# A two-layer linear-attention block: phi(q) loaded with its 32-token blocks side by side, M's rows in a matching order, the square's high part on ScalarE

## The chip, the cores and the metric

The kernel runs on one NeuronCore of a Trainium2 chip. The metric is the device time of one execution in microseconds (us). A kernel's time is the median of several executions. The profile is one further execution, recorded by the hardware profiler; its span goes from the first to the last instruction, and its own time is a little longer than the span.

## What is computed

The input x has 2048 tokens of 640 features in float32. Two layers, with the same weights, each do:

```
phi(t) = where(t > 0, t + 1, exp(t)) + 1e-6
q, k, v = layernorm(x) @ wqkv                      # 32 heads of 20
kv = phi(k)^T v  per head;   z = sum over tokens of phi(k)
o  = (phi(q) kv) / (phi(q) . z + 1e-6)             # per head
x  = x + o @ wo
h  = relu(layernorm(x) @ w1 + b1)
x  = x + (h * h) @ w2 + b2                         # 640 -> 1728 -> 640
```

The kernel merges the block-diagonal kv with wo: M = kv @ wo is a 640 x 640 matrix, and the attention output is (phi(q) / den) @ M.

Nearly all matmuls multiply float32 values in three passes. Each operand is split into a high part (rounded to the matmul's type) and a low part (the value less its high part), and high x low, low x high and high x high are summed in PSUM. So each operand of a matmul costs one copy (high) and one subtraction (low) on other engines.

## The kernel before

**Tiling.** The 2048 tokens are 16 tiles of 128 (`NT`), the 640 features are 5 chunks of 128 (`DC`), the 1728 hidden features 14 chunks (`NF`, the last of 64). For the feed-forward part the tiles go in 4 groups of 4 (`TG`, `NG`).

**Stages of a layer.** First the k and q projections over all tiles, with the sums for kv; phi(q) of each tile is stored to memory (`pqd[t]`), for some tiles in "late" quarters (`late_q`, each 15 matmuls of 320 columns) that are placed later as work for TensorE. Then the transition: the sum z is spread over all partitions (`zbc`), kv and M are made (`kv_make`, `m_make`), M is split into high and low (`m_split`), and the first four tiles (group 0) are projected through M, added to x and normalised. Then the feed-forward part, group by group: for each of 14 chunks `fc1` (15 matmuls of 512 columns), `act` (Relu, square, split), and `fc2` of the chunk before (15 matmuls of 512). Beside group g's chunks the kernel does the attention output of group g+1, two tiles at a time, by a scheme of seven products instead of eight (`Pair`, `p1` to `p7`), which takes sums and differences of M's row chunks and of the turned phi(q).

**What sets the order.** The order is written by hand: each engine works through its instructions in the order in which the program emits them. Beside the feed-forward part, `pair_plan`, `fast`, `OUT0`, `OUTS` and `STRIP` say at which chunk and at which place of it ("pre", after the i-th tile of `fc2`, "pe", "post") each step of a pair is emitted (`side`, `run`). All DMAs but one are issued by SyncE, in program order, and a DMA that waits holds up those behind it. The tiles come from rings; `ftile` is one of 12 tiles of 128x640.

**phi(q) of a tile, from memory to the projection.** `b_load_pq` loads the stored tile, tokens on partitions. `b_ops` multiplies it by `zbc` (L626), sums per head (L629), adds and inverts (L635, L636), scales the tile (L638), and turns it: a projection needs features on partitions. `blocks_T` (L375) is one VectorE transpose, which turns each 32x32 block in place; `blocks_move` then puts the 16 blocks of a 128x128 square where they belong, with 16 ScalarE copies of 32 partitions x 160 per tile (L388). The result is split by `split` or `p_split`. The moves are handed out in quarters (`side_moves` and `run_side` in the transition, `moves0` and `moves1` of a plan in the feed-forward part). The normalised tiles that feed `fc1` go through the same two steps; these stay as they are.

**M.** `m_make(c)` makes 120 rows of M (6 heads; 40 rows for the last of 6 pieces) in PSUM; ScalarE copies them out. Piece 0 goes straight into `m_raw[0]`; the others go to an `ftile` and are laid into the 128-row tiles `m_raw[0..4]` by one or two DMAs each:

```
m, r = divmod(o, P)
k = min(P - r, n)
nc.sync.dma_start(m_raw[m][r : r + k], u[:k])
if k < n:
    nc.sync.dma_start(m_raw[m + 1][: n - k], u[k:n])
```

`m_split(m)` makes the high part (L984) and the low part (L985), both on VectorE. The first projections use M[0] to M[2] (`proj(..., range(3))`), then M[3] and M[4]. Between the pieces and behind them stand late quarters: one after piece 2, two after piece 5. Eight subtractions of M's halves (`m_sums`) feed the seven-product scheme, four on GpSimd and four on VectorE.

**act.** ScalarE takes the Relu from PSUM (L1141), VectorE squares it (L1142), casts the high part (L1143) and takes the low part (L1144).

Of the kernel before, what the change touches and what calls it, by code (L numbers as in the profile page):

```python
# [13 lines left out]
P = 128  # L14
# [33 lines left out]
def pair_plan(b, m0, m1, turn, out, back):  # L48

    return {"moves0": m0, "moves1": m1, "turn": turn, "out": out, "back": back}  # L50


def fast(b, m0=None, m1=None):
    return pair_plan(
        b, m0 or (b - 3, 0), m1 or (b - 2, 0), [(b - 1, 0), (b - 1, 1), (b - 1, 2), (b - 1, 3)],
        {"p1": (b, 0), "p4": (b, 1), "p6": (b, 2), "p7": (b, 3), "p5": (b, 4),
         "p2": (b + 1, 0), "p3": (b + 1, 2)},
        [((b, "post"), (b + 1, 0), (b + 1, 1), (b + 2, 0), (b + 2, 1), (b + 2, 3)),
         ((b + 1, 3), (b + 1, "post"), (b + 2, 0), (b + 2, "post"), (b + 3, "pre"), (b + 3, 4))],
    )  # L60
# [7 lines left out]
OUTS = ({**fast(2), ("den", 1): ((-1, 1), (-1, 3))}, fast(9))  # L68
# [7 lines left out]
def kernel(  # L76
# [87 lines left out]
    def utile(name):  # L164
        return tmp.tile([P, 2 * D], R32, tag="u", name=name, bufs=RING)

# [288 lines left out]
    for layer in range(N_LAYERS):  # L455
# [167 lines left out]
        def b_ops(t):  # L623

            pr = ftile("pr")
            nc.vector.tensor_tensor(out=pr, in0=pq[t], in1=zbc, op=ALU.mult)  # L626
# [14 lines left out]
            yield  # L641
            yzp[t] = blocks_T(pq.pop(t))
# [13 lines left out]
        def b_split(t, u):  # L656
            split(u[:, 0], u[:, 1], yzp.pop(t)[1])
            pT[t] = chunks(u)
# [4 lines left out]
        def b_x1(t, ps, n=0):  # L663
            v = halves_sb(xr[t])
            nc.vector.tensor_tensor(out=v, in0=halves(ps), in1=v, op=ALU.add)
            if n:
                m_sum(n, xr[t][:, :1])
            b_norm(t)

        def b_norm(t):  # L670
            ln_stats(("b", t), xr[t])
            next(m_vec)
            xn[t] = ftile("xn")
            ln_apply(("b", t), xn[t], xr[t])
# [198 lines left out]
        zbc = tmp.tile([P, D], F32, tag="z", name="zbc", bufs=1)  # L873
# [6 lines left out]
        for j in range(2):  # L880
            nc.scalar.activation(zbc[:, j * HD : (j + 1) * HD], psz[j], AF.Copy)
# [16 lines left out]
        def side_moves(yz, then=None):  # L898
            side_work.extend(lambda k=k: blocks_move(yz, (k,)) for k in range(P // B32))
            if then:  # L900
                side_work.append(then)
# [33 lines left out]
        def m_make(c):  # L935
            mb.append(mb.pop(0))
            ps = bank(mb[-1], 2)
            n, o = head_rows(c), HR * c
            for j in range(2):
                nc.tensor.matmul(  # L940
                    ps[:n, j * 512 : j * 512 + HD], kvbd[c][:n, :n],
                    vo["o", c][:n, j * HD : (j + 1) * HD], start=True, stop=True,
                )

            u = m_raw[0] if c == 0 else ftile("Mc")
            nc.scalar.activation(halves_sb(u[:n]), halves(ps[:n]), AF.Copy)
            if c > 0:
                m, r = divmod(o, P)
                k = min(P - r, n)
                nc.sync.dma_start(m_raw[m][r : r + k], u[:k])  # L950
                if k < n:
                    nc.sync.dma_start(m_raw[m + 1][: n - k], u[k:n])

        def m_sums(m, engine):


            b1, b2, lo, hi = m_raw[m], m_raw[m + 2], slice(0, HD), slice(HD, D)
            for out, x, y in (
                (b1[:, lo], b1[:, hi], b1[:, lo]),
                (b1[:, hi], b2[:, hi], b1[:, hi]),  # L960
                (b2[:, hi], b2[:, hi], b1[:, lo]),
                (b2[:, lo], b2[:, lo], b2[:, hi]),
            ):
                engine.tensor_tensor(out=out, in0=x, in1=y, op=ALU.subtract)
                yield


        m_pool, m_vec = m_sums(0, nc.gpsimd), m_sums(1, nc.vector)
        W = (2, 1, 1, 0, 0)

        def m_sum(n, v):

            w = small.tile([P, 1], F32, tag="rs", name="rs")
            nc.gpsimd.tensor_copy(w, v)
            for _ in range(n):
                next(m_pool)

        def split_sum(t, n):
            u = xtile("pT")
            b_split(t, u)  # L980
            m_sum(n, u[:, 1, :1].bitcast(F32))

        def m_split(m):
            nc.vector.tensor_copy(M[m][:, 0], m_raw[m])  # L984
            nc.vector.tensor_tensor(  # L985
                out=M[m][:, 1], in0=m_raw[m], in1=M[m][:, 0].bitcast(F32), op=ALU.subtract
            )
# [24 lines left out]
        side_moves(yzp[2], lambda: split_sum(2, W[0]))  # L1012
# [12 lines left out]
        m_split(2)  # L1025
        late_q(1)
        run_side(1)
        m_split(3)

# [11 lines left out]
        for i in range(2):  # L1041
            po[i] = bank(4 + 2 * i, 2)
            proj(po[i], pT[i], M, range(3))
            if i == 0:
                m_split(4)
            run_side(2)
# [7 lines left out]
        def x_there(i):  # L1054
            f_split(i, yzx.pop(i)[1])
            if i == 0:
                m_sum(W[2], xTb[0][:, 1, 0, :1].bitcast(F32))

# [12 lines left out]
        for i in (2, 3):  # L1071
# [3 lines left out]
            b_x1(i, po[i], W[i + 1])  # L1075
            if i == 2:
                xbanks = [1, 2, 3]
            late_q(1)
            run_side(1)
        late_q(1)  # L1080
# [24 lines left out]
        )  # L1105

# [28 lines left out]

        def act(c, ps):
# [3 lines left out]
            if c < 13:  # L1140
                nc.scalar.activation(r, ps, AF.Relu, bias=b1sb[:, c : c + 1])  # L1141
                nc.vector.tensor_tensor(out=r, in0=r, in1=r, op=ALU.mult)  # L1142
                nc.vector.tensor_copy(h[:, 0], r)  # L1143
# [141 lines left out]
        def x1_tile():  # L1285
            return bp.tile([P, TG, D], F32, tag="x1", name="x1", bufs=1)

        def x1_load(g):
            x1s[g] = x1_tile()
# [4 lines left out]
        if layer == 0:  # L1294
            stage = x1_tile()
# [13 lines left out]
        def s_turns(t):  # L1309


            z0, z1 = yzp.pop(t)[1], yzp.pop(t + 1)[1]
# [20 lines left out]
        def p_split(t, first=0):  # L1333

            u = bp.tile([P, 2, D], R32, tag="pT", name="pT", bufs=2)
            v, s = yzp[t][1], slice(first * P, D)
# [125 lines left out]
        def side(g, p, plan, at):  # L1462

            t0, t1 = TG * g + 2 * p, TG * g + 2 * p + 1
            m0, m1, turn, out, back = plan["moves0"], plan["moves1"], plan["turn"], plan["out"], plan["back"]
            for t, (s, pl) in ((t0, m0), (t1, m1)):
                if t != TG:
                    at(s - 4, "post", lambda t=t: b_load_pq(t))
                den, blk = plan.get(("den", t - t0), ((s - 2, "post"), (s - 1, 1)))
                at(*den, lambda t=t: b_den(t))  # L1470
                at(*blk, lambda t=t: b_blocks(t))
                for k in range(4):
                    at(s + (pl + k) // 5, (pl + k) % 5, lambda t=t, k=k: blocks_move(yzp[t], (k,)))
            steps(at, lambda: p_split(t0), (m0[0] + 1, 0), (m0[0] + 1, 4))
            steps(at, lambda: p_split(t1, 2), (m1[0] + 1, 0), (m1[0] + 1, 1))
# [71 lines left out]

        pend = None
        for g in range(NG):
            for c in range(NF):  # L1550
# [4 lines left out]
                if last_layer and g == NG - 1 and c == NF - 2:  # L1555
                    hl = act(c + 1, fc1(g, c + 1, spare=True))
                    fc2(*pend)
# [3 lines left out]
                if pend:  # L1561
                    fc2(*pend, after=lambda i: run(g, c, i))
                    wu.load_ring()
                else:
                    for i in range(TG + 1):
                        run(g, c, i)
# [6 lines left out]
                if g == 0 and c < TG:  # L1573
                    f_bias(c)
# [38 lines left out]
```

## Time and profile before

| | us |
|---|---|
| median of 3 runs | 1345.48 |
| the three runs | 1344.94, 1345.48, 1345.90 |
| the profiled execution's own time | 1345.11 |
| its span | 1343.4 |
| first layer's feed-forward part begins | 252.67 |
| second layer's M begins | 874.21 |

How to read the lines below. The engines are PE (TensorE), PEld (its weight loads), DVE (VectorE), ACT (ScalarE), POOL (GpSimd) and SP (SyncE). In the page's first part stand busy time, share of the span and number of instructions of each. A group of instructions reads: line, engine, operation, output<-input by the program's names, shapes, count | busy us, mean ns of one | idle time before them and what ended it. A line of the timeline reads: start, duration, engine, line, operation, names and shapes, count, and in brackets the idle time before it with its releaser. A line of the stretches reads: from:to and length, then busy time and instructions of PE, PEld, DVE, ACT and POOL, the granted clock, the share of the DMA engines and GB/s. A line of TensorE's waits reads: who waited for whom, us in total, times, the longest. A DMA line reads: names, queue, count, KB of one, median us from issue to landing. A matmul's duration includes its way through the array, so matmuls overlap: their spacing is shorter than their duration.

### The profile page before, as it was taken

To read this page: it belongs to the slowest core of one execution; us is meant where nothing else is said; L and a number is where in the kernel's file an instruction comes from. 1 tells how busy PE (TensorE), PEld (TensorE's weight loads), DVE (VectorE), ACT (ScalarE), POOL (GpSimd) and SP (SyncE) were. 2 spreads that over 40 slices of the span, in tenths; PEclk is the share of its full clock that TensorE was granted. 3 is DMA by queue.
4 is the path that set the end of the run, shared out by engine and by line. 5 is a ranking of instruction groups with operands and counts; after the bars stand their busy time and mean duration, and the time that the engine had idled before them with its cause. 6 is when DMAs were issued, how large, how long until landed. Compare 5 with 4: busy or idle time off the path is not lost.

```text
span 1343.4 us, 19060 instructions
## 1 busy us (share of the span) xinstructions
PE 1336.3 (99%) x6746; PEld 1151.6 (86%) x6746; DVE 937.6 (70%) x1711; ACT 788.7 (59%) x1996; POOL 133.1 (10%) x185
## 2 busy tenths in 40 slices
PE   9999999999999999999999999999999999999998
PEld 8888999988888888888888899998888888888887
DVE  8888868887876776643467678678769767666323
ACT  5878848666647548512647686495657466474120
POOL 2222210100000000000012232110000000000000
PEclk9999999999999999999999999999999999999999
DMA  6787825474565575487621115156546556555635
GB/s 206 256 302 269 286 88 181 159 295 168 182 220 175 184 268 171 156 307 278 223 98 50 50 40 156 42 207 232 180 168 240 180 183 214 212 169 185 243 132 192
DMA packets 85637, 253.44 MB, mean 189 GB/s; under 512 B 11030, under 2 KB 19606, under 8 KB 84902
## 3 DMA queue, kind: packets, MB, share of 16 engines
q1 hardware_dynamic: 85398, 252.04, 53.7%
q8 instruction: 53, 0.87, 0.3%
q14 instruction: 42, 0.34, 0.1%
q10 hardware_dynamic: 144, 0.20, 0.0%
HBM read 193.50 MB, written 56.03 MB: 186 GB/s over the span
## 4 chain that ended last, share of the span: by engine, by line
PE 90%; DVE 7%; ACT 1%; DMA 1%; issue 1%; POOL 0%; SPq 0%; DVEq 0%
PE PS L400 36%; PE PS L1179 24%; PE PS L1130 24%; PE PS L421 2%; PE PS L927 1%; PE PS L940 1%; ACT z L388 1%; PE PS L736 1%; DVE y L375 1%; DMA pqt<-pq 1%; DVE hr L1142 0%; DVE x L1230 0%; DVE bn L355 0%; DVE pqt L638 0%; DVE pr L626 0%
## 5 line engine op out<-in xcount | busy, mean ns | idle before, releaser
L388 ACT ACTIVATE z<-y 32x160 f32<-32x160 f32 x1384 | 462.5, 334 | 65.2 <-DVE y L375 48.7
L1130 PE MATMUL PS<-xTb,u 128*128 128x512 f32 x1400 | 333.4, 390 | 0.6 <-DVE hr L1150 0.6
L1130 PEld LDWEIGHTS PS<-xTb,u 128*128 128x128 f32 x1400 | 262.0, 188 | 55.6 <-DVE hr L1150 1.5
L400 PE MATMUL PS<-kq,xT 128*128 128x320 f32 (+2 forms) x1575 | 284.5, 335 | 0.0
L1179 PE MATMUL PS<-u,h 128*128 128x512 f32 x1120 | 279.4, 390 | 0.0
L400 PEld LDWEIGHTS PS<-kq,xT 128*128 128x128 f32 x1575 | 250.3, 188 | 27.8 <-DVE rl L506 1.5
L1179 PEld LDWEIGHTS PS<-u,h 128*128 128x128 f32 x1120 | 207.9, 188 | 40.0
L1141 ACT ACTIVATE hr<-PS,b1sb 128x512 f32<-128x512 f32 x104 | 71.4, 686 | 276.0 <-PE PS L1130 275.2
L1142 DVE TENSOR_TENSOR hr<-hr 128x512 f32<-128x512 f32 x104 | 71.6, 688 | 186.2 <-ACT hr L1141 186.2
L400 PE MATMUL PS<-kh,xh 128*128 128x512 f32 x480 | 124.1, 392 | 0.0
L498 ACT ACTIVATE e<-PS 128x320 f32<-128x320 f32 (+4 forms) x128 | 53.5, 435 | 107.7 <-PE PS L400 99.3
L359 POOL TENSOR_SCALAR rs<-mv 128x1 f32<-128x1 f32 x63 | 29.7, 472 | 755.9 <-DVE mv L357 755.9
L400 PEld LDWEIGHTS PS<-kh,xh 128*128 128x128 f32 x480 | 87.1, 188 | 15.2 <-DVE kh L700 0.4
L505 DVE TENSOR_SCALAR e<-e 128x320 f32<-128x320 f32 (+4 forms) x128 | 41.6, 325 | 70.1 <-ACT e L498 69.9
L1179 PE MATMUL PS<-h,u 128*128 128x512 f32 x280 | 79.4, 391 | 0.2
L1144 DVE TENSOR_TENSOR h<-hr,h 128x512 fp32r<-128x512 f32 x104 | 72.0, 693 | 3.6
L697 POOL TENSOR_TENSOR acc<-acc,r 128x640 f32<-128x640 f32 x30 | 53.9, 1796 | 197.6 <-DVE r L506 197.6
L1179 PEld LDWEIGHTS PS<-h,u 128*128 128x128 f32 x280 | 51.9, 188 | 11.6 <-DVE strip L1195 1.0
L1130 PE MATMUL PS<-xTb,uw 128*128 128x512 f32 x240 | 57.0, 389 | 0.0
L506 DVE SCALAR_TENSOR_TENSOR r<-PS,e 128x512 f32<-128x512 f32 (+2 forms) x104 | 51.1, 491 | 5.8 <-ACT e L498 2.4
L1130 PEld LDWEIGHTS PS<-xTb,uw 128*128 128x128 f32 x240 | 45.1, 188 | 9.4
L1143 DVE CAST h<-hr 128x512 fp32r<-128x512 f32 x104 | 44.4, 427 | 7.8 <-DVE hr L1142 0.5
(137 smaller groups left out, 1525.7 us busy)
## 6 DMA issues: line engine op xcount, KB each, us to landing
u<-kept_w SPq DMA_DIRECT2D x184, 640.0 KB, 4.8
x<-x SPq DMA_DIRECT2D x48, 320.0 KB, 4.5
kept_w<-uprep SPq DMA_DIRECT2D x23, 640.0 KB, 5.3
pqt<-pq SPq DMA_DIRECT2D x32, 320.0 KB, 5.1
x<-xr SPq DMA_DIRECT2D x32, 320.0 KB, 2.4
st<-in_B_w_dram SPq DMA_DIRECT2D x22, 320.0 KB, 5.2
pq<-r SPq DMA_DIRECT2D x20, 320.0 KB
kept_kq<-kq SPq DMA_DIRECT2D x10, 640.0 KB, 5.8
```

The costliest lines, as they stand in the source:

```text
L388: nc.scalar.activation(d, v, AF.Copy)
L400: nc.tensor.matmul(ps, a, b, start=first and i == 0, stop=last and i == 2)
L498: nc.scalar.activation(self.e[:, a:b], ps, AF.Exp)
L505: nc.vector.tensor_scalar(e, e, 1.0, PHI_EPS, op0=ALU.min, op1=ALU.add)
L506: nc.vector.scalar_tensor_tensor(out=self.r[:, a:b], in0=ps, scalar=0.0, in1=e, op0=ALU.max, op1=ALU.add)
L697: nc.gpsimd.tensor_tensor(out=acc, in0=acc, in1=r, op=ALU.add)
L1130: nc.tensor.matmul(ps, a[:, d, :], bb[:, d, :], start=n == 0, stop=n == len(order) - 1)
L1141: nc.scalar.activation(r, ps, AF.Relu, bias=b1sb[:, c : c + 1])
L1142: nc.vector.tensor_tensor(out=r, in0=r, in1=r, op=ALU.mult)
L1143: nc.vector.tensor_copy(h[:, 0], r)
L1144: nc.vector.tensor_tensor(out=h[:, 1], in0=r, in1=h[:, 0].bitcast(F32), op=ALU.subtract)
L1179: nc.tensor.matmul(ps, l, r, start=first and k == 0, stop=last and k == len(a) - 1)
```

## The change

- `b_load_pq` loads a tile by four DMAs. Partition 32j + q gets, from tokens q, 32 + q, 64 + q and 96 + q, the features 160j to 160j + 159, side by side. The arithmetic of `b_ops` keeps its shapes in other views; `zbc` holds only the 160 sums that its partition needs, written in four pieces by ScalarE and VectorE.
- One VectorE transpose with a strided input then gives the whole turned tile, and the 16 ScalarE moves are gone for phi(q). Row 32j + b of feature chunk c now holds feature 160j + 32c + b instead of 128c + 32j + b.
- M's rows are put in the same order: each run of up to 32 rows of a piece goes by a DMA of its own to `m_raw[m][32j + ...]`. All six pieces go this way.
- `m_split`'s high part is made by ScalarE. The late quarters that stood between M's pieces and splits stand differently: none after piece 2, two right behind piece 5 and one behind the first three splits. All `m_sums` are on VectorE.
- `act`: ScalarE makes the square's high part directly from the Relu (function Square). VectorE's square and low part are emitted later, after the second tile of the following `fc2` (`LOW_AT`).
- The plans change: the first group's pairs start at chunks 4 and 9 instead of 5 and 10, the strips at chunk 6 instead of 8, and the slots for moves of phi(q) are gone. The `x1` tile and the first `pT` tile of the feed-forward pool are allocated when the pool opens.

The order of TensorE's matmuls changes with the plans and the late quarters; their number and shapes don't.

```diff
-OUT0 = (fast(5), {**fast(10, (5, 0), (8, 0)), ("vec", 0): (0,)})
+OUT0 = (fast(4), fast(9))
-STRIP = ((8, 0), (8, 2), (8, 4), (9, 0), (9, 2))
+STRIP = ((6, 0), (6, 2), (6, 4), (7, 0), (7, 2))
...
+    JB = P // B32
+    R_ = D // JB
...
         def b_load_pq(t):
                 pq[t] = ftile("pqt")
-                nc.sync.dma_start(pq[t], pqd[t])
+                v = pqd[t].rearrange("(i q) (j r) -> j q i r", i=JB, j=JB)
+                for j in range(JB):
+                    nc.sync.dma_start(
+                        pq[t][j * B32 : (j + 1) * B32].rearrange("q (i r) -> q i r", i=JB), v[j]
+                    )
...
-            nc.vector.tensor_tensor(out=pr, in0=pq[t], in1=zbc, op=ALU.mult)
+            nc.vector.tensor_tensor(
+                out=pr.rearrange("p (i r) -> p i r", i=JB),
+                in0=pq[t].rearrange("p (i r) -> p i r", i=JB),
+                in1=zbc[:, None, :].to_broadcast([P, JB, R_]), op=ALU.mult,
+            )
...
-            yzp[t] = blocks_T(pq.pop(t))
+            yzp[t] = z = ftile("z")
+            nc.vector.transpose(
+                out=z, in_=pq.pop(t).rearrange("p (i c b) -> p c i b", i=JB, b=B32)
+            )
...
-        side_moves(yzp[0], lambda: b_split(0, xtile("pT")))
+        b_split(0, xtile("pT"))
         b_den(1)
-        run_side(4)
         b_blocks(1)
-        side_moves(yzp[1], lambda: b_split(1, xtile("pT")))
+        side_work.append(lambda: b_split(1, xtile("pT")))
...
-            u = m_raw[0] if c == 0 else ftile("Mc")
+            u = ftile("Mc")
             nc.scalar.activation(halves_sb(u[:n]), halves(ps[:n]), AF.Copy)
...
+            r = o
+            while r < o + n:
+                k, b = divmod(r, B32)
+                l = min(B32 - b, o + n - r)
+                j, m = divmod(k, DC)
+                nc.sync.dma_start(m_raw[m][j * B32 + b : j * B32 + b + l], u[r - o : r - o + l])
+                r += l
...
         def m_split(m):
-            nc.vector.tensor_copy(M[m][:, 0], m_raw[m])
+            nc.scalar.activation(M[m][:, 0], m_raw[m], AF.Copy)
...
+        Q = (2, 1, 1, 1)
         for c in range(NH):
             m_make(c)
-            run_side(1)
+            if c > 2:
+                run_side(1)
             b_step(3)
-            if c == 2:
-                late_q(1)
-            if c in (3, 4):
-                m_split(c - 3)
-        side_moves(yzp[3], lambda: split_sum(3, W[1]))
+        side_work.append(lambda: b_split(3, xtile("pT")))
+        late_q(Q[0])
+        run_side(1)
+        for m in range(3):
+            m_split(m)
         late_q(1)
-        run_side(1)
-        m_split(2)
-        late_q(1)
-        run_side(1)
         m_split(3)
+        m_split(4)
+        m_sum(4)
...
             if c < 13:
                 nc.scalar.activation(r, ps, AF.Relu, bias=b1sb[:, c : c + 1])
-                nc.vector.tensor_tensor(out=r, in0=r, in1=r, op=ALU.mult)
-                nc.vector.tensor_copy(h[:, 0], r)
-                nc.vector.tensor_tensor(
-                    out=h[:, 1], in0=r, in1=h[:, 0].bitcast(F32), op=ALU.subtract
-                )
+                nc.scalar.activation(h[:, 0], r, AF.Square)
+
+                def rest():
+                    nc.vector.tensor_tensor(out=r, in0=r, in1=r, op=ALU.mult)
+                    nc.vector.tensor_tensor(
+                        out=h[:, 1], in0=r, in1=h[:, 0].bitcast(F32), op=ALU.subtract
+                    )
+
+                lows.append(rest)
```

More of the change, by code (lines that the diff above doesn't have):

```diff
@@ L671, in b_norm @@
             ln_stats(("b", t), xr[t])
-            next(m_vec)
+            m_sum(1)
             xn[t] = ftile("xn")
@@ L872 @@
         late_q(1)
-        zbc = tmp.tile([P, D], F32, tag="z", name="zbc", bufs=1)
+        zbc = tmp.tile([P, R_], F32, tag="z", name="zbc", bufs=1)
         psz = [xbank()[:, :HD] for _ in range(2)]
@@ L879 @@
                 )
-        for j in range(2):
-            nc.scalar.activation(zbc[:, j * HD : (j + 1) * HD], psz[j], AF.Copy)
+        for j in range(JB):
+            p, k = slice(j * B32, (j + 1) * B32), j % 2
+            v = psz[j // 2][p, k * R_ : (k + 1) * R_]
+            if k == 0:
+                nc.scalar.activation(zbc[p], v, AF.Copy)
+            else:
+                nc.vector.tensor_copy(zbc[p], v)
         b_den(0)
@@ L963, in m_sums, with m_sum @@
             ):
-                engine.tensor_tensor(out=out, in0=x, in1=y, op=ALU.subtract)
+                nc.vector.tensor_tensor(out=out, in0=x, in1=y, op=ALU.subtract)
                 yield
[L968 to L974, printed above, removed]
-            for _ in range(n):
[L976 to L981, printed above, removed]
+        m_turn = [m_sums(m) for m in range(2)]
+        def m_sum(n):
+            for _ in range(n):
+                next(m_turn[0])
         def m_split(m):
-            nc.vector.tensor_copy(M[m][:, 0], m_raw[m])
+            nc.scalar.activation(M[m][:, 0], m_raw[m], AF.Copy)
             nc.vector.tensor_tensor(
@@ L1105, with x1_tile, pT_tile @@
         )
+        def x1_tile():
+            return bp.tile([P, TG, D], F32, tag="x1", name="x1", bufs=1)
+        def pT_tile():
+            return bp.tile([P, 2, D], R32, tag="pT", name="pT", bufs=2)
+        x1_first, pT_first = [x1_tile()], [pT_tile()]
         def fresh(nm):
@@ L1134, in fc1, with low @@
             return ps
+        lows = []
+        def low():
+            if lows:
+                lows.pop(0)()
         def act(c, ps):
@@ L1333, in p_split @@
         def p_split(t, first=0):
-            u = bp.tile([P, 2, D], R32, tag="pT", name="pT", bufs=2)
-            v, s = yzp[t][1], slice(first * P, D)
+            u = pT_first.pop() if pT_first else pT_tile()
+            v, s = yzp[t], slice(first * P, D)
             nc.scalar.activation(u[:, 0, s], v[:, s], AF.Copy)
@@ L1464, in side @@
             t0, t1 = TG * g + 2 * p, TG * g + 2 * p + 1
-            m0, m1, turn, out, back = plan["moves0"], plan["moves1"], plan["turn"], plan["out"], plan["back"]
-            for t, (s, pl) in ((t0, m0), (t1, m1)):
+            m0, m1, turn, out, back = plan["blocks0"], plan["blocks1"], plan["turn"], plan["out"], plan["back"]
+            for t, s in ((t0, m0), (t1, m1)):
+                den, blk = plan.get(("den", t - t0), ((s - 1, "post"), (s, 1)))
                 if t != TG:
-                    at(s - 4, "post", lambda t=t: b_load_pq(t))
-                den, blk = plan.get(("den", t - t0), ((s - 2, "post"), (s - 1, 1)))
+                    at(den[0] - 2, "post", lambda t=t: b_load_pq(t))
                 at(*den, lambda t=t: b_den(t))
                 at(*blk, lambda t=t: b_blocks(t))
[L1472 to L1475, printed above, removed]
+            steps(at, lambda: p_split(t0), (m0 + 1, 0), (m0 + 1, 2))
+            steps(at, lambda: p_split(t1, 2), *plan.get("split1", ((m1 + 1, 0), (m1 + 1, 1))))
             steps(at, lambda: s_turns(t0), *turn)
@@ L1546, in side_last, with after @@
                 blocks_move(yz0[2], (2 * c - 24, 2 * c - 23))
+        def after(g, c, i):
+            if i == LOW_AT:
+                low()
+            run(g, c, i)
         pend = None
@@ L1565 @@
                     for i in range(TG + 1):
-                        run(g, c, i)
+                        after(g, c, i)
                 pend = g, c, h
```

66 lines of the change are left out of this document (30 added, 36 removed).

## The prediction

> **What bounds the kernel now.** I read the busy times first, then TensorE's own waits, then the few stretches that contain them.
>
> ```profile
> PE 1336.3 (99%) x6746; PEld 1151.6 (86%) x6746; DVE 937.6 (70%) x1711; ACT 788.7 (59%) x1996; POOL 133.1 (10%) x185
> ...
> PE PS L544 <- POOL ident masks.py:199: 1.4, 1, 1.4
> PE PS L400 <- DVE xr L1390: 0.8, 1, 0.8
> PE PS L1130 <- DVE hr L1150: 0.6, 2, 0.3
> ...
> 268.80:302.40 33.60, 32.79 (x160) 27.88 (x160) 28.05 (x51) 21.75 (x56) 0.79 (x2) 1.00 0.76 295
> 336.00:369.60 33.60, 33.27 (x159) 27.95 (x158) 27.89 (x51) 21.37 (x57) 1.58 (x4) 1.00 0.53 184
> 369.60:403.20 33.60, 33.49 (x166) 28.46 (x165) 24.70 (x46) 16.06 (x42) 1.58 (x4) 1.00 0.60 218
> 1008.00:1041.60 33.60, 33.19 (x148) 26.82 (x147) 30.65 (x55) 25.38 (x68) 0.79 (x2) 1.00 0.67 243
> 1310.40:1343.40 33.00, 29.20 (x131) 23.85 (x129) 11.62 (x20) 3.35 (x5) 0.00 (x0) 1.00 0.54 189
> ```
>
> TensorE is busy for 1336.3 of 1343.4 us, so 7.1 us are idle. The last stretch (33.00 less 29.20) holds 3.8 us, mostly the tail after the last matmul, and 1.6 us are waits at the start (1.4 for the identity and 0.2 for the first normalised tile). What is left for any change of order is 0.81 + 0.33 + 0.11 + 0.41 = 1.7 us. The change adds and removes no matmul; it moves the order of a few. So a lighter VectorE or ScalarE can buy at most about 1.7 us (0.13%), while any wait put in TensorE's way costs its full length. The whole question is whether the change makes such a wait.
>
> **Parts that lie beside other work.** These rows price them:
>
> ```profile
> L388 ACT ACTIVATE z<-y 32x160 f32<-32x160 f32 x1384 | 462.5, 334 | 65.2 <-DVE y L375 48.7 <-DMA x<-x 0.6
> L1141 ACT ACTIVATE hr<-PS,b1sb 128x512 f32<-128x512 f32 x104 | 71.4, 686 | 276.0 <-PE PS L1130 275.2
> L1143 DVE CAST h<-hr 128x512 fp32r<-128x512 f32 x104 | 44.4, 427 | 7.8 <-DVE hr L1142 0.5
> L375 DVE STREAM_TRANSPOSE y<-pqt 128x640 f32<-128x640 f32 x32 | 27.0, 844 | 1.0
> L964 POOL TENSOR_TENSOR Mr<-Mr 128x320 f32<-128x320 f32 x8 | 7.0, 880 | 0.5 <-DMA u<-kept_w 0.3
> pqt<-pq SPq DMA_DIRECT2D x32, 320.0 KB, 5.1
> ```
>
> Of the 1384 block moves, 504 go: 504 x 0.334 = 168 us off ScalarE. It gets 104 squares; the trace has no square, so between a cast's 0.43 (on another engine) and the Relu's 0.69 from PSUM; I take 0.69, 72 us. VectorE loses 104 x 0.427 = 44 us of casts and gets the eight 128x320 subtractions, which GpSimd did in 0.88 each (7 us at most). All of this lies under TensorE, which waits for neither engine except in the stretches above. The transpose now reads runs of 32 elements 160 apart. The trace has no such read: 0.84 us if the pattern is free, twice that if not; I take 0.84, because the ScalarE moves already read 32-wide pieces. The upper value would add 32 x 0.84 = 27 us to an engine that idles for 1343 - 938 = 406.
>
> Each load of a phi(q) tile becomes four DMAs of 32 partitions, 96 more on SyncE's queue. Landing took 5.1 us before and the loads are issued about two chunks (14 us) ahead of their use; at 0.4 to 0.9 us of issue each (rows below) a tile is complete 1.2 to 2.7 us later. The tight one is the second tile of group 1 in layer 0, whose chain ends in the 0.8 us wait on L1390. Its deadline moves up one chunk, but four slots of block moves leave the chain, so I keep that wait as it is (0 to 2.5 us).
>
> [...]
>
> The waits on L1150 (0.6 us) sit at the turn to group 1 in both layers, where VectorE is busiest; the plan of that pair ends one chunk earlier now and has 0.43 us less per chunk. I give the change the idle of those stretches, 0.33 + 0.11 + 0.41, so -0.9 us.
>
> **The part on the path: M's rows.** M is made in six pieces of 120 rows (40 in the last). Before, the first is copied straight into place and the others are laid into 128-row tiles by 9 DMAs per layer. Now the rows of each tile come from all over M, and no piece is copied straight: 4+5+5+4+4+2 = 24 DMAs per layer, all issued by SyncE one after the other. TensorE and SyncE in layer 0, and what the edits touch:
>
> ```profile
> 206.75 2.46 PE L400 MATMUL PS<-kq,xT 128*128 128x320 f32 x15
> 209.05 3.39 PE L940 MATMUL PS<-uraw,kvbd 120*120 120x320 f32 x12
> 217.93 4.67 PE L400 MATMUL PS<-kq,xT 128*128 128x320 f32 x30
> 222.44 13.40 PE L421 MATMUL PS<-uM,pT 128*128 128x320 f32 x90
> ...
> 210.33 0.70 ACT L946 ACTIVATE Mr<-PS 120x640 f32<-120x640 f32 x1 [0.64 <-PE PS L940]
> ...
> 200.43 0.49 DVE L506 SCALAR_TENSOR_TENSOR rl<-PS,e 128x320 f32<-128x320 f32 x1
> 200.84 0.81 DVE L626 TENSOR_TENSOR pr<-pqt,zbc 128x640 f32<-128x640 f32 x1
> 207.25 0.81 DVE L134 TENSOR_TENSOR pT<-z,pT 128x640 fp32r<-128x640 f32 x1
> 209.72 0.33 DVE L505 TENSOR_SCALAR e<-e 128x320 f32<-128x320 f32 x1 [0.32 <-ACT e L498]
> 210.08 0.49 DVE L506 SCALAR_TENSOR_TENSOR rl<-PS,e 128x320 f32<-128x320 f32 x1
> ...
> 210.60 0.33 SPq L867 DMA_DIRECT2D pq<-rl  x1
> 212.90 0.74 SPq L950 DMA_DIRECT2D Mr<-Mc  x1
> 213.70 0.61 SPq L952 DMA_DIRECT2D Mr<-Mc  x1
> 215.03 0.53 SPq L950 DMA_DIRECT2D Mr<-Mc  x1
> 215.61 0.87 SPq L952 DMA_DIRECT2D Mr<-Mc  x1
> 217.48 0.78 SPq L950 DMA_DIRECT2D Mr<-Mc  x1
> 218.31 0.55 SPq L952 DMA_DIRECT2D Mr<-Mc  x1
> 219.61 0.56 SPq L950 DMA_DIRECT2D Mr<-Mc  x1
> 220.26 0.83 SPq L952 DMA_DIRECT2D Mr<-Mc  x1
> ...
> Mr<-Mc SPq DMA_DIRECT2D x2, 240.0 KB, 2.8
> Mr<-Mc SPq DMA_DIRECT2D x2, 80.0 KB, 3.9
> ...
> L985 DVE TENSOR_TENSOR uM<-Mr,uM 128x640 fp32r<-128x640 f32 x10 | 8.3, 825 | 0.3
> L133 ACT ACTIVATE uT<-Mr 128x640 fp32r<-128x640 f32 x8 | 5.2, 730 | 0.0
> ```
>
> The deadline. TensorE makes M from 209.05 and starts the first projection at 222.44. Between these lie 45 late matmuls before and after, only placed differently, so the deadline stays 13.4 us after M's first matmul.
>
> The cost of an issue. In order, the rows are of 8, 112, 16, 104, 24, 96, 32 and 88 partitions. Those of 16, 32, 96 and 112 held SyncE 0.53 to 0.61 us, the others 0.74 to 0.87, while the store of the row above them took 0.33. From start to start this is about 0.58 for 16 partitions (215.03 to 215.61), 0.65 for 32 (219.61 to 220.26), 0.80 for 8, 0.83 for 24.
>
> When the queue starts. The first piece is copied at 211.03 (210.33 + 0.70). But the store in front on SyncE (210.60) waits for the late quarter's `rl` on VectorE (ready 210.57), and that comes later now: the low half of tile 0's phi(q) is taken right after 200.84 and waits there for ScalarE's high half (about 0.65), then costs 0.75 start to start; tile 1's takes the place it had at 207.25. Of these 1.4 us, 0.3 fall into VectorE's idle at 209.72. So `rl` is ready at 211.6, and the first M DMA starts at 212.05.
>
> When M[0] is there. Its last 32 rows are rows 480 to 511, the first DMA of the fifth piece, 19th in the queue. The 18 ahead of it: first piece 3 x 0.65 + 0.83 = 2.8; second 0.80 + 3 x 0.65 + 0.58 = 3.3; third the same 3.3; fourth 2.8; sum 12.2. It starts at 224.3 and lands 2.8 us later (the median of the 96-row DMA; the one 32-row value is 3.9), at 227.1. ScalarE's high part takes 0.73, so the projection starts at about 227.9 instead of 222.44: 5.4 us of idle TensorE. The low part (0.83 on VectorE) is wanted four matmuls, 0.6 us, later: 0.25 more. M[1] and M[2] follow one DMA (0.65) each, faster than the six matmuls each feeds (0.9). M[3] and M[4] are there by about 231.5 and wanted at 233. **5.7 us per layer, 11.4 for two**: layer 1's rows have the same issue times and the same 13.4 us.
>
> Both ends: if each issue cost the 0.33 + 0.05 of the ordinary store, the 19th would start at 212.05 + 18 x 0.38 = 218.9, land at 221.7 and be ready, high part included, at 222.4: no stall. With the landing of 3.9 it is 6.8 per layer, 13.6. I take 0.65 because a DMA of exactly this shape and direction shows it. Behind the queue stand the weight loads of the ring (issued from 223.9 before, about 4.5 us later now), first wanted 25 us on: covered.
>
> [...]
>
> **Sum**, on the profiled execution's 1345.11 us (span 1343.4 and 1.7 around it): + 11.4 - 0.9 = 1355.6. The three runs' median is 0.4 above the profiled one: **1356 us**, 0.8% slower.
>
> **Rivals.**
>
> *The gather is hidden (chance 0.18).* It has the 0.33 us store for it, and the order, which puts three late quarters in one row ahead of the projection. Then only the 0.9 us gain shows: 1344.6, at best 1343.8 with all 1.7. It decides from an issue interval of about 0.38 us downwards. Against it stand nine DMAs, none under 0.53.
>
> *The stall also slows TensorE's clock (0.24).*
>
> ```profile
> 1.41 4.80 PE L544 MATMUL PS<-ident 128*128 128x128 f32 x22 [1.41 <-POOL ident masks.py:199]
> 246.80 0.71 PE L369 MATMUL PS<-ident,xn 128*128 128x128 f32 x5
> ```
>
> After the idle start, 22 small matmuls took 4.80 us, 0.21 each, where later ones pass at about 0.11: 2.3 us lost, though the granted clock reads 1.00. No wait in the trace is longer than 1.4 us, so whether 5.7 us of idle brings the slow start back is not shown. If it does, each stall costs 2.3 more: 1358 with one, 1360.6 with both. [...]
>
> *ScalarE's squares make the feed-forward part wait (0.08).* Where a normalised tile is turned back, one chunk holds Relu 0.69, square 0.69, two high parts of 0.74 and 16 moves of 0.334: 8.2 us against a chunk of 6.8. The next Relu is 1.4 late and has 3.4 us (the second half of a chunk) before its PSUM bank is wanted. It decides if VectorE's turn comes 2 us later; at 0.5 us in 12 places it adds 6: 1362.
>
> *VectorE alone doesn't do it (inside the forecast).* The strided transpose at twice the price stays under TensorE, as above.
>
> **How the numbers follow.** Forecast 0.50, at 1356, with its own range 1352 (issues at 0.58, and the store in front no later than now) to 1358 (landing 3.9). Rivals 0.18, 0.24 and 0.08. The range runs from the hidden gather's 1344.4 to 1361, both stalls with a slow clock. Below 0.2% (2.7 us) a measurement of this kernel can't be told from no change. Faster by more than that needs more than the 1.7 us there are: 0.04. The rest of the hidden case is no change: 0.14. Slower: 0.82.
>
> **What would show it.** Right: in both layers a wait of TensorE at the first projection, released by ScalarE's high part of M (new line 998), behind a row of 24 SyncE issues about 0.6 us apart; feed-forward stretches without idle. The queue's row wrong: issues at 0.35 us. The clock rival: the first projection matmuls after the wait at twice their spacing. Wrong altogether: no wait there, or waits on the Relu's bank (L1130 before).

## The result, and the profile after

| | before | after |
|---|---|---|
| median of 5 runs, us | 1344.94 | 1357.24 |
| lowest to highest | 1344.80 to 1345.90 | 1356.71 to 1358.72 |
| ratio after to before, with its 95% interval | | 1.0091 [1.0076, 1.0106] |
| profiled execution: time, span | 1345.11, 1343.4 | 1358.72, 1356.7 |

The changed kernel is 0.9% slower. First the changed kernel's page: the busy times, and three of its rows, two groups of instructions and the DMAs of phi(q)'s tiles.

```profile
PE 1339.3 (99%) x6746; PEld 1155.2 (85%) x6746; DVE 891.4 (66%) x1601; ACT 694.1 (51%) x1606; POOL 124.4 (9%) x171
...
L398 ACT ACTIVATE z<-y 32x160 f32<-32x160 f32 x880 | 294.0, 334 | 60.8 <-DVE y L385 50.9
...
L1169 ACT ACTIVATE h<-hr 128x512 fp32r<-128x512 f32 x104 | 65.8, 633 | 3.3
...
pqt<-pq SPq DMA_DIRECT2D x128, 80.0 KB, 4.9
```

The engines that the change was to relieve are relieved: ScalarE works 95 us less (788.7 to 694.1; 504 moves of 0.334 gone, 104 squares of 0.633 and M's ten high parts come), VectorE 46 us less. TensorE has the same 6746 matmuls and 3 us more of busy time. Its idle time has grown from 7.1 to 17.4 us (1356.7 less 1339.3). TensorE's waits, in us in total, times, and the longest, say where:

```profile
PE PS L431 <- ACT uM L998: 8.8, 2, 4.6
...
PE PS L1210 <- DVE h L1173: 0.8, 1, 0.8
PE PS L755 <- ACT xT L576: 0.8, 1, 0.8
PE PS L410 <- ACT su L1425: 0.6, 1, 0.6
PE PS L410 <- DVE xr L1418: 0.2, 1, 0.2
...
```

The first row is the new one: the first projection through M (L431) waits in both layers for the high part of M (L998). The old waits on VectorE's `hr` at the turn to group 1 are gone. The timelines of the changed kernel around M: TensorE in layer 0 and in layer 1, then SyncE's queue and ScalarE in layer 0, and VectorE's new transpose:

```profile
209.41 6.74 PE L962 MATMUL PS<-uraw,kvbd 120*120 120x320 f32 x24
216.09 6.86 PE L410 MATMUL PS<-kq,xT 128*128 128x320 f32 x45
227.58 14.96 PE L431 MATMUL PS<-uM,pT 128*128 128x320 f32 x90 [4.63 <-ACT uM L998]
242.37 2.36 PE L410 MATMUL PS<-kq,xT 128*128 128x320 f32 x15
...
899.08 15.27 PE L431 MATMUL PS<-uM,pT 128*128 128x320 f32 x90 [4.19 <-ACT uM L998]
914.18 1.04 PE L410 MATMUL PS<-kq,xT 128*128 128x320 f32 x6
...
211.91 0.33 SPq L886 DMA_DIRECT2D pq<-rl  x1
212.28 16.33 SPq L974 DMA_DIRECT2D Mr<-Mc  x24
228.71 1.37 SPq L886 DMA_DIRECT2D pq<-rl  x1
...
226.79 2.07 ACT L998 ACTIVATE uM<-Mr 128x640 fp32r<-128x640 f32 x3 [4.94 <-DMA Mr<-Mc]
...
199.56 0.84 DVE L661 STREAM_TRANSPOSE z<-pqt 128x640 f32<-128x640 f32 x1
```

M is computed by 216.1 and the 45 late matmuls end at about 222.9. Then TensorE stands still until 227.58, because SyncE is still issuing the 24 DMAs that put M's rows in place: 16.33 us, 0.68 us each. The 19th began at 224.66; ScalarE took M[0] at 226.79 (it had landed after 2.06 us) and TensorE went on with the high part of M[0].

There is a second loss in the same place. From the start of the projection to the next late matmuls its 90 matmuls took 14.79 us (227.58 to 242.37) and 15.10 us (899.08 to 914.18); before it was 13.23, from 222.44 to the late matmuls here:

```profile
235.67 0.60 PE L400 MATMUL PS<-kq,xT 128*128 128x320 f32 x3
```

The changed kernel's stretches, with TensorE's busy time behind the length and the granted clock third from the end, show why, in layer 0 and in layer 1:

```profile
220.65:224.07 3.42, 2.29 (x16) 2.03 (x14) 1.55 (x3) 1.06 (x2) 0.00 (x0) 1.00 0.37 83
224.07:227.48 3.41, 0.00 (x0) 0.00 (x0) 0.00 (x0) 0.69 (x1) 0.00 (x0) 1.00 0.60 134
227.48:230.90 3.42, 3.32 (x12) 3.32 (x13) 3.31 (x6) 2.47 (x6) 0.00 (x0) 0.50 0.35 88
230.90:234.31 3.41, 3.41 (x25) 3.41 (x24) 3.02 (x6) 0.71 (x1) 0.00 (x0) 1.00 1.05 332
...
896.50:899.91 3.41, 0.83 (x4) 0.59 (x4) 0.85 (x2) 1.62 (x3) 0.00 (x0) 1.00 0.51 114
899.91:903.32 3.41, 3.41 (x14) 3.38 (x14) 3.38 (x6) 2.11 (x4) 0.00 (x0) 0.50 0.77 225
```

For 3.42 us after the wait in layer 0 the granted clock is 0.50, and 12 matmuls pass where 25 pass in the next stretch. A busy share near 100% says nothing of this: TensorE's 3 us of added busy time are mostly these slow matmuls.

Counted by the starts of the same matmuls in the two traces, after less before, the loss comes together so:

| part of the span | us |
|---|---|
| up to M (start of the program) | +0.36 |
| layer 0: wait for M | +4.78 |
| layer 0: first projection, 14.79 instead of 13.23 | +1.56 |
| layer 0: from there to its end | +0.44 |
| layer 1: wait for M and first projection | +6.23 |
| layer 1: turn to group 1 | -1.06 |
| all the rest (0.7 of it behind the start of the last feed-forward matmul) | +1.0 |
| span, 1343.4 to 1356.7 | +13.3 |

The +0.44 is a loss and a gain. At the turn to group 1 TensorE gained about 1.1 us, in both layers, and in layer 0 the old wait of 0.8 us on `xr` went too. Against these, layer 0 lost 2.4 us ahead of the turn, counted against the first experiment below, which has the same matmuls behind the projection and no wait there: three waits of 0.8, 0.6 and 0.2 us (L1210, and L410 for `su` and `xr`), and wider spacing of the matmuls around them. Their cause in the trace is one tile of phi(q). The lines on the tile `pqt` from 258 to 280 us (line, operation, count, shortest, median and longest ns, first and last start; then the time from the last issue to landing):

```profile
L629 SPq DMA_DIRECT2D pqt<-pq x4: 430/431/588, 265.5 to 266.9; - x4
DMA to landing us min/median/max: 9.4/9.4/9.4
```

And VectorE's timeline, at its instruction that wanted the tile:

```profile
276.43 0.83 DVE L640 TENSOR_TENSOR pr<-pqt,zbc 128x640 f32<-128x640 f32 x1 [4.03 <-DMA pqt<-pq]
```

The four loads of this tile were issued 5.1 us later than the one load before (265.5 against 260.4), no later than everything else after the first stall: the feed-forward part began 6.7 us later. What was late is the landing, 9.4 us after the last issue. VectorE stood for 4.03 us at it, what the program has behind it came after that, and TensorE's next `h` and `su` were late. In the six experiments the loads of these tiles landed after 5.8 to 8.2 us, VectorE waited 0.9 to 2.2 us for this one, and TensorE waited for neither `h` nor `su`. Why it took 9.4 us here isn't shown. The profiled execution is the slowest of the five, 1.5 us above their median; that the others lost less here fits, but their traces weren't recorded.

### The profile page after: what moved, and what is told of

The parts are those of the page before. It is cut to its first block, busy times and chain, and to the rows that moved or that the text cites. A ratio compares the mean times of both kernels' runs of the same rounds, so it can differ in the third digit from the quotient of the medians.

```text
span 1356.7 us, 18757 instructions
## 1 busy us (share of the span) xinstructions
PE 1339.3 (99%) x6746; PEld 1155.2 (85%) x6746; DVE 891.4 (66%) x1601; ACT 694.1 (51%) x1606; POOL 124.4 (9%) x171
## 4 chain that ended last, share of the span: by engine, by line
PE 92%; DVE 3%; DMA 2%; SPq 1%; ACT 1%; issue 1%; POOL 0%; DVEq 0%; ACTq 0%
PE PS L410 35%; PE PS L1210 27%; PE PS L1150 26%; PE PS L431 2%; DMA pqt<-pq 1%; PE PS L949 1%; PE PS L962 1%; SPq L974 1%; PE PS L755 0%; ACT z L398 0%; DMA st<-in_A_wqkv_dram 0%; DVE bn L365 0%; DMA Mr<-Mc 0%; DVE e L515 0%; DVE r L516 0%
## 5 line engine op out<-in xcount | busy, mean ns | idle before, releaser
L398 ACT ACTIVATE z<-y 32x160 f32<-32x160 f32 x880 | 294.0, 334 | 60.8 <-DVE y L385 50.9
L410 PE MATMUL PS<-kq,xT 128*128 128x320 f32 (+2 forms) x1575 | 283.6, 334 | 0.0
L1210 PE MATMUL PS<-u,h 128*128 128x512 f32 x1120 | 279.9, 390 | 0.8 <-DVE h L1173 0.8
L410 PEld LDWEIGHTS PS<-kq,xT 128*128 128x128 f32 x1575 | 250.1, 188 | 27.5 <-issue 1.4
L1210 PEld LDWEIGHTS PS<-u,h 128*128 128x128 f32 x1120 | 207.8, 188 | 40.9 <-DVE h L1173 1.2
L410 PE MATMUL PS<-kh,xh 128*128 128x512 f32 x480 | 124.1, 392 | 0.1
L410 PEld LDWEIGHTS PS<-kh,xh 128*128 128x128 f32 x480 | 87.1, 188 | 15.3 <-DVE kh L719 0.4
L1210 PE MATMUL PS<-h,u 128*128 128x512 f32 x280 | 79.1, 390 | 0.0
L1169 ACT ACTIVATE h<-hr 128x512 fp32r<-128x512 f32 x104 | 65.8, 633 | 3.3
L1210 PEld LDWEIGHTS PS<-h,u 128*128 128x128 f32 x280 | 52.0, 188 | 10.5 <-DVE h L1186 0.4
L1418 DVE TENSOR_TENSOR xr<-PS,xr 128x320 f32<-128x320 f32 x48 | 23.5, 489 | 51.1 <-PE PS L410 49.8
```

Of the source, the lines that this page charges most:

```text
L398: nc.scalar.activation(d, v, AF.Copy)
L410: nc.tensor.matmul(ps, a, b, start=first and i == 0, stop=last and i == 2)
L1169: nc.scalar.activation(h[:, 0], r, AF.Square)
L1210: nc.tensor.matmul(ps, l, r, start=first and k == 0, stop=last and k == len(a) - 1)
```

## The experiments

The theory: TensorE waits for the gather because its issues take over 0.6 us each in one queue, and the slow clock after the wait comes on top. The rivals: the projection is slow for another reason (its operands, the low parts of M), the late quarters in the way are what delays it, or other parts of the change cost time too.

**Is it the clock?** 34 transposes of 128x128 without use stand ahead of the first projection, in both layers, so that TensorE has work during the wait.

```diff
+        for _ in range(34):
+            nc.tensor.transpose(bank(3)[:, :P], ident, ident)
         for i in range(2):
             po[i] = bank(4 + 2 * i, 2)
```

> The changed kernel (1357.2 us) with 34 extra 128x128 transposes of the identity into a free PSUM bank, put in TensorE's queue right before the first projection of both layers; the gather of M is untouched. In the profile of the changed kernel TensorE waits 4.6 and 4.2 us there and then runs at a granted clock of 0.51 for 3.4 us. Theory (the wait costs its length, and the slow clock behind it costs more on its own): the extra transposes end before M's high part is there, so the first real projection matmul starts at the same time, but the 90 projection matmuls take 13.3 instead of 14.8 and 15.1 us: about 1.5 us less per layer, 1354.3 us, and no stretch with a clock below 1. Rival (the projection is slow after the wait because M's parts arrive late one by one): the 90 matmuls stay at 14.8 us or more, time 1357.

Measured: 1355.28 us (1354.26 to 1356.37), ratio 1.0075 [1.0060, 1.0090], 1.0 us above what the theory expected. TensorE's waits in this run:

```profile
PE PS L431 <- ACT uM L998: 2.5, 2, 1.5
```

Its timeline at the projections of layer 0 and layer 1:

```profile
222.40 3.87 PE L1057 MATMUL PS<-ident 128*128 128x128 f32 x34
227.22 13.74 PE L431 MATMUL PS<-uM,pT 128*128 128x320 f32 x90 [0.94 <-ACT uM L998]
240.79 2.36 PE L410 MATMUL PS<-kq,xT 128*128 128x320 f32 x15
...
896.11 13.75 PE L431 MATMUL PS<-uM,pT 128*128 128x320 f32 x90 [1.52 <-ACT uM L998]
909.69 2.36 PE L410 MATMUL PS<-kq,xT 128*128 128x320 f32 x15
```

M[0] comes at the same time as without them (227.22 against 227.58); only what fills it differs. The 90 matmuls take 13.57 us (227.22 to 240.79) and 13.58 us in layer 1, instead of 14.79 and 15.10, and the mean granted clock of this execution is 0.999 against 0.997 in the changed kernel's. So the slow clock costs 1.2 and 1.5 us, 2.7 together, in the profiles, and 0.34 over the 13.23 of before are left. They are the wait for the low part of M[0], which is ready at 228.02 in this trace; the fifth matmul, the first to use it, starts at 228.08. So M's parts account for that much, and are out as the cause of the rest. By the medians the kernel gained 2.0 us, and the interval of this ratio overlaps that of the changed kernel; it is the trace that tells the two apart.

**Is it the one queue?** Six of the 24 DMAs go to ScalarE's queue; nothing else changes.

```diff
+        SCALAR_K = {0: (3,), 1: (6, 7), 2: (10, 11), 3: (14,)}
...
-                nc.sync.dma_start(m_raw[m][j * B32 + b : j * B32 + b + l], u[r - o : r - o + l])
+                eng = nc.scalar if k in SCALAR_K.get(c, ()) else nc.sync
+                eng.dma_start(m_raw[m][j * B32 + b : j * B32 + b + l], u[r - o : r - o + l])
```

> The changed kernel with six of the 24 DMAs per layer that lay M's rows into place issued by ScalarE instead of SyncE (those of row blocks 3; 6 and 7; 10 and 11; 14). Theory (SyncE's issue time, some 0.63 us from one start to the next, sets when M[0] is whole): 12 instead of 18 DMAs are ahead of M[0]'s last one on SyncE, so it starts about 3.8 us earlier; TensorE's wait before the projection falls from 4.6 and 4.2 us to below 1, below the length that slows the clock, and the time falls by about 2 x 5.4 us to 1346.5. Rival 1 (the DMA engines or the landing set it): the wait stays above 3.5 us, time 1356 or more. Rival 2 (the issues now in ScalarE's queue hold up its copies of M's pieces and the high parts): the wait falls by less than 2 us, time 1353 to 1356.

Measured: 1347.25 us (1346.03 to 1348.44), ratio 1.0015 [1.0005, 1.0024]. TensorE's waits in this run:

```profile
PE PS L963 <- ACT Mc L969: 1.1, 2, 0.8
...
PE PS L431 <- ACT uM L1000: 0.4, 1, 0.4
```

The timelines of SyncE, ScalarE (with the DMAs it issues, ACTq) and TensorE in layer 0:

```profile
212.53 12.82 SPq L976 DMA_DIRECT2D Mr<-Mc  x18
...
211.73 1.36 ACTq L976 DMA_DIRECT2D Mr<-Mc  x1
213.27 0.70 ACT L969 ACTIVATE Mc<-PS 120x640 f32<-120x640 f32 x1 [1.57 <-DMA Mr<-Mc]
214.01 1.31 ACTq L976 DMA_DIRECT2D Mr<-Mc  x2
...
216.18 1.27 PE L963 MATMUL PS<-uraw,kvbd 40*40 40x320 f32 x4 [0.81 <-ACT Mc L969]
```

10 of the 12.3 us are back. But ScalarE also copies M's pieces out of PSUM (L969), and an issue in its queue holds the next copy: 1.36 us for one DMA, 1.31 for two. TensorE's next piece of M then waits for a PSUM bank, 1.1 us in all.

**Would later quarters help?** Four late quarters instead of two follow the last piece of M, so that TensorE has 30 more matmuls while the gather goes on.

```diff
-        Q = (2, 1, 1, 1)
+        Q = (4, 1, 0, 0)
```

> The changed kernel with two more late quarters (2 x 2.28 us of TensorE work) put ahead of the first projection and two fewer behind it. Theory: the wait at the projection falls to about 0.3 us and the clock stays, but the work taken away covered the chain from the projection's result over normalising and turning to the next transposes; in the kernel before, that chain ended within 0.1 us of its use, so a new wait of 2 to 4 us per layer stands there: 1350 to 1354 us. Rival (there was slack in that chain, since VectorE has less to do there): no new wait, 1345 us.

Measured: 1354.46 us (1352.26 to 1355.10), ratio 1.0066 [1.0051, 1.0081]: just over what the theory expected, and far from the rival's 1345. TensorE's waits in this run:

```profile
PE PS L379 <- DVE xn L375: 5.7, 2, 2.8
PE PS L431 <- ACT uM L998: 1.5, 1, 1.5
```

Stretches of this run in layer 0, with the columns as above:

```profile
247.13:250.54 3.41, 1.46 (x10) 1.20 (x9) 2.80 (x6) 3.30 (x10) 0.73 (x2) 1.00 0.04 11
250.54:253.95 3.41, 2.52 (x11) 2.52 (x12) 3.09 (x8) 3.31 (x9) 0.19 (x1) 0.50 0.25 96
253.95:257.37 3.42, 3.42 (x15) 3.38 (x15) 2.52 (x5) 0.47 (x2) 0.92 (x2) 0.50 0.00 0
257.37:260.78 3.41, 3.41 (x23) 3.23 (x22) 1.93 (x5) 1.58 (x3) 0.00 (x0) 1.00 0.00 0
```

The quarters cover the gather but for 1.5 us in layer 0. They are then missing where they stood: after the projection TensorE waits 2.8 us per layer for the normalised tile (L375). And this shorter wait slows the clock for 6.83 us, twice as long as the wait of 4.6 us did. The wait was moved, not covered.

**Is it the gather alone?** M's rows go where they went before, one or two DMAs a piece and the first piece straight into place; all the rest of the change stays. The run leaves out the matching of M's rows to phi(q)'s new order, so its output is not the block's, and only its time is read.

```diff
-            u = ftile("Mc")
+            u = m_raw[0] if c == 0 else ftile("Mc")
...
-            r = o
-            while r < o + n:
-                k, b = divmod(r, B32)
...
+            if c > 0:
+                m, r = divmod(o, P)
+                k = min(P - r, n)
+                nc.sync.dma_start(m_raw[m][r : r + k], u[:k])
+                if k < n:
+                    nc.sync.dma_start(m_raw[m + 1][: n - k], u[k:n])
```

> The changed kernel with M's rows laid down as in the kernel before: piece 0 copied straight into place, the others by 9 DMAs per layer (so the permutation of M's rows is left out). Theory (of the added 12.3 us the gather of M makes 12.4, by the wait and the slow clock behind it, and everything else cancels): no wait at the projection in either layer, clock 1.00 throughout, 1344.8 us, within 0.2% of the kernel before. Rival (the loads of phi(q) in four parts, the ScalarE high parts of M or the squares carry part of it): 1347 us or more.

Measured: 1343.61 us (1343.06 to 1344.94), ratio 0.9989 [0.9979, 0.9998]. Of TensorE's waits only these are left, both at the start of the program:

```profile
PE PS L554 <- POOL ident masks.py:199: 1.4, 1, 1.4
PE PS L755 <- ACT xT L576: 0.2, 1, 0.2
```

And TensorE's timeline at the projection in layer 0:

```profile
222.72 13.75 PE L431 MATMUL PS<-uM,pT 128*128 128x320 f32 x90
236.30 2.36 PE L410 MATMUL PS<-kq,xT 128*128 128x320 f32 x15
```

So everything in the change but the order of M's rows gains 0.11%, some 1.5 us, and the gather costs 1.0091 - 0.9989 = 1.02%, some 13.7 us. The projection takes 13.58 us here as well (222.72 to 236.30), so its 0.34 us over the kernel before come from the rest of the change and not from the gather: the splits of M now come right ahead of the projection. M[0]'s low part is ready at 223.51 and the fifth matmul starts at 223.56, where the kernel before had that low part at 219.73, ahead of the whole projection.

**Can the gather be hidden?** Five DMAs of the later pieces go to ScalarE, which by then has fewer copies to make, and SyncE's late store of phi(q) is held until the gather is issued.

```diff
+        SCALAR_K = {1: (6,), 2: (10,), 3: (12, 13, 14)}
...
                 if j == 1:
-                    nc.sync.dma_start(pqd[t], late_phi.pop(t).r)
+                    r = late_phi.pop(t).r
+                    if hold:
+                        held.append((t, r))
+                    else:
+                        nc.sync.dma_start(pqd[t], r)
...
+        hold.clear()
+        for t, r in held:
+            nc.sync.dma_start(pqd[t], r)
```

> The changed kernel with five of the 24 DMAs of M issued by ScalarE, now few after the first three pieces (row blocks 6; 10; 12, 13 and 14), so that its copies of these keep up with TensorE's three PSUM pairs, and with SyncE's store of the late quarter in front of the gather moved behind it. Theory: 13 DMAs at 0.65 us ahead of M[0]'s last one, from 211.5 instead of 212.3, so it starts near 220 and M[0]'s high part is there near 222.9, when TensorE comes: waits of at most 0.5 us per layer at the projection and none of the 0.8 us waits for ScalarE's copies; 1344.0 to 1344.8 us, 0 to 0.1% below the kernel before. Rival (any issue in ScalarE's queue delays its copies as in the first split of the gather): 1346 to 1347.

Measured: 1345.12 us (1344.29 to 1350.02), against 1344.97 for the kernel before in the same comparison; ratio 1.0003 [0.9994, 1.0013]. TensorE's wait at the projections in this run:

```profile
PE PS L431 <- ACT uM L1004: 0.6, 2, 0.4
```

SyncE's timeline in layer 0:

```profile
211.26 13.19 SPq L980 DMA_DIRECT2D Mr<-Mc  x19
```

The new waits of the first split are gone and the clock stays at 1.00, so 12 of the 12.3 us come back. It ends 0.3 us above the expected range, and equal to the kernel before: the queue still takes 0.69 us an issue, and 0.6 us of wait remain. One of its eleven executions took 1350.02 us, at a mean granted clock of 0.997 where the others had 0.999 or 1.000; it has no trace. No run with M's rows in phi(q)'s order beats the kernel before.

**Does the number of issues decide, or their rows?** The runs of up to 32 rows are cut at 16, so that the same bytes go in 43 DMAs per layer.

```diff
-                l = min(B32 - b, o + n - r)
+                l = min(16 - b % 16, o + n - r)
```

> The changed kernel with M's rows laid down by DMAs of up to 16 rows instead of 32: 43 per layer instead of 24, the same bytes to the same places, all on SyncE. Theory (the count of issues sets the wait): 33 DMAs stand ahead of M[0]'s last one instead of 18, 29 of them at 0.58 and 4 at 0.75 us from start to start, 19.8 us instead of 12.4; the wait at the projection is 7.4 us longer in each layer, about 12 us, and the slow clock behind it stays of the same size: 1372 us. Rival (bytes, the DMA engines or the landing set the wait): within 2 us of 1357.

Measured: 1375.79 us (two runs, 1373.36 and 1378.22), ratio 1.0229 [1.0211, 1.0248]. TensorE's wait at the projections in this run:

```profile
PE PS L431 <- ACT uM L998: 27.5, 2, 13.7
```

SyncE's timeline in layer 0:

```profile
211.80 27.90 SPq L974 DMA_DIRECT2D Mr<-Mc  x43
```

Stretches of layer 0, the last of the wait and the first of the projection:

```profile
232.46:235.87 3.41, 0.00 (x0) 0.00 (x0) 0.00 (x0) 0.46 (x1) 0.00 (x0) 0.50 0.32 65
235.87:239.28 3.41, 3.08 (x11) 3.08 (x12) 2.21 (x3) 2.07 (x4) 0.00 (x0) 0.50 0.29 59
```

43 issues took 27.90 us, 0.65 each, against 0.68 each for the 24: half the rows do not make an issue cheaper, so the count sets the length of the queue. The wait is 13.7 us per layer, where the theory expected about 12 (and 1372 us in all) and the changed kernel has 4.4. The clock is at half during the wait too (0.50 from 225.63), where that costs nothing, and for 3.1 us of work behind it.

## Why the prediction was right

The sign, the place and the mechanism were right, and 1357.24 lies beside the 1356 forecast. The two agree more closely than the terms do.

- *What bounds the kernel*: right. Relief of 95 us on ScalarE and 46 us on VectorE bought 1.5 us (the run with M's rows as before), inside the bound of 1.7. I gave it 0.9. But the 1.5 is a net: by the starts of the same matmuls in that run and in the kernel before, the two feed-forward parts became 2.7 us shorter (1.85 and 0.83), and the start and the transitions 1.0 us longer, 0.7 of it in the two projections. So the idle time of the stretches was not all that there was to gain, and the bound held by luck.
- *The light parts*: hidden, as said. The square from the Relu cost 0.633 us where 0.69 was taken; the strided transpose 0.84, as taken, so the pattern is free. The rival in which ScalarE's squares make the feed-forward part wait is out: without the gather there is no such wait.
- *The tight tile of group 1*: I kept its wait at 0.8 us with an upper end of 2.5. In the profiled execution the three waits were 1.6 us and cost 2.4, by a load in four parts that landed late. Among the waits of the six experiments none of TensorE for `h` or `su` stands, so the size is that of one execution.
- *The gather*: the queue was right. The 19th DMA began at 224.66, and 224.3 was worked out, on a stage that was 0.36 us later as a whole. Its landing was mis-sized: 2.06 us, where 2.8 was taken from a DMA of 96 rows. So the wait was 4.6 and 4.2 us instead of 5.4 per layer. The 0.25 for the low part, measured 0.3, was put to the gather, but the run without the gather has it too.
- *The clock*: here the likeliest case was wrong. It had TensorE go on at full speed after the stall, and the slow clock stood as a rival with a chance of 0.24. It came true in both layers. Its size of 2.3 us per stall, taken from the start of the program, was too large: 1.2 and 1.5 us, by the run with the transposes. The granted clock of 1.00 that was read at that start tells nothing: in the stored trace of the kernel before, the record of the clock begins only at 5.93 us, when those 22 matmuls (1.41 to 6.21) are nearly over.

By terms of the forecast, against the run without the gather: the waits are 9.1 us by the starts of the same matmuls (4.8 and 4.35), where 11.4 was forecast with the low parts in it; the gain is 1.5, with the low parts' 0.7 already taken off, where 0.9 was forecast; and the clock, 2.7 us, was missing. These misses (-2.3, -0.6 and +2.7) nearly cancel, which is luck. The three terms give 10.3 us where the time rose by 12.3, so some 2 us are in none of them. In the profiled execution the trace has 2.4 us at the late tile and 0.7 behind the start of the last feed-forward matmul; how much of these the other executions have stays open, and no experiment isolates them. One figure of the range does not follow from its working: its lower end is 1344.4, where the hidden gather was summed to 1344.6.

Not tried: a gather through memory, M made with its rows already in the new order, or fewer and larger DMAs.

## What to carry to other kernels

A permutation that is "only DMAs" was priced here by its number of issues in one queue, not by its bytes: with 24 DMAs TensorE waited 4.4 us per layer, with 43 for the same bytes 13.7. Count them, multiply by the issue time of the same kind of DMA in the trace, and compare with when the consumer starts. The issues moved to ScalarE's queue were paid in its own instructions (1.36 us for one, 1.31 for two, ahead of the next copy), so give them to an engine that nobody waits for at that time. Behind TensorE's waits of 4.63 and 4.19 us the granted clock was 0.50 for 3.41 us and cost 1.2 and 1.5 us more: add such a loss to the price of a wait, and look at the granted clock, not at the busy share.

## What the runs showed of the hardware

- An issue on SyncE from one SBUF tile to another took 0.65 us on average at up to 16 rows and 0.68 at up to 32, where the store of phi(q) to memory took 0.33 (the row at 211.91). The next store, right behind the 24 (the row at 228.71), took 1.37, so the kind of DMA is not all that counts. Why they differ isn't known from these runs.
- The granted clock was 0.50 for 3.41 us in either layer of the changed kernel (from 227.48 and from 899.91 us), for 6.83 in layer 0 of the run with four late quarters (from 250.54) and for 13.65 in layer 0 of the run with 43 DMAs (from 225.63). TensorE's waits at these places were 4.63, 4.19, 2.84 and 13.73 us. So a wait of 2.84 us came with more slow time than one of 4.63, and the length of the wait alone does not tell it. In the 3.41 us before the clock fell, TensorE had worked for 0.00, 0.83, 1.46 and 0.25 us; in the 3.41 to 3.42 us before it rose, for 3.32, 3.41, 3.42 and 3.08. In the changed kernel 3.42 us with 2.29 of work (from 220.65) were followed by full clock, in the run with four late quarters 3.41 us of half clock with 2.52 of work (from 250.54) by more half clock. The waits of 0.78 us in the changed kernel (L1210) and of 0.81 in the kernel before (L400 on `xr`) lie in stretches with a clock of 1.00. What makes the clock fall and rise isn't known from these runs.
